# Turning -max one step later and putting four fill products behind the first key scores of a burst

## The chip, the cores and the metric

The kernel runs on one core of one Trainium2 chip. The metric is the device time of one execution, in microseconds (us); the times of before are three runs, and one more execution was recorded by the hardware profiler.

## The reference

Two independent results are joined along the last axis. Sequence length S is 2048, width D is 1024, there are 32 heads of width 32, and all heads share one set of keys and values. Everything is float32.

```python
# A: attention
q = (x @ wq).reshape(B, S, H, Dh).transpose(0, 2, 1, 3)
k = x @ wk
v = x @ wv
scores = einsum("bhqd,bkd->bhqk", q, k) * (Dh ** -0.5)
p = softmax(scores, axis=-1)
a = einsum("bhqk,bkd->bhqd", p, v).transpose(0, 2, 1, 3).reshape(B, S, H * Dh) @ wo
# B: Fourier mixing, real part
fa = einsum("bsd,ed->bse", xb, dft_hid_re);  fb = einsum("bsd,ed->bse", xb, dft_hid_im)
b = einsum("ts,bse->bte", dft_seq_re, fa) - einsum("ts,bse->bte", dft_seq_im, fb)
return concatenate([a, b], axis=-1)
```

## The kernel before

**Two streams on TensorE.** The attention proper is cut into 32 units (4 blocks of 512 queries times 8 groups of 4 heads) and each unit into 32 steps. All other matrix products (the projections of q, the Fourier part, the output projection) are the *fill*: float32 products made of three products of high and low halves each, `rh`/`rl` times `mh`/`ml`, 128x512 in size, written to the two one-bank PSUM pools that appear as `psb`. A group of 12 or 24 fill products adds up in one bank; when a group ends, VectorE copies or adds the bank out. `take(n)` issues the next n fill products, `pos["fill"]` counts them, and transfers and casts for later fill are issued when the count comes near their due position (`pump`).

**What one step does.** A step n of the main loop issues, in this order: `score_step(n + 44)`, `expo(n)`, and fill up to a level.

- `score_step` calls `ask`, which issues the *query scores* of a step 44 ahead (`scores`: two products `pss<-kst,qst` with the queries on the partitions, and VectorE's `TENSOR_REDUCE nm<-pss`, which gives -max per query), and ScalarE's exponential with row sums of the query scores before them (`pss<-pss,nm`). The pool `ps_s` of `pss` has two buffers.
- `expo(n)` issues the *key scores*: two products `pst<-qst,kst` with the keys on the partitions, and ScalarE's `p<-pst`, the exponential that the product with v needs. The pool `ps_t` of `pst` has one buffer, so the next key scores wait until this exponential has read it.
- At every eighth step (r % 8 == 0) three fill products, one more `ask`, and then `pv` follow: 16 products `psb<-p,v` with v (32 rows in the trace), into the `psb` bank that no open group holds, read out by VectorE (`ov`).

I call the eight steps from one `pv` to the next a *burst* and number the steps in it 0 to 7 (n % 8): `pv` ends step 0. T1, T2, T3 are the key scores of steps 1, 2 and 3. In step 1 no new query scores are issued, as step 0 has issued two sets.

**Turning -max.** The exponentials by keys need -max of each query as a row, which the query scores give as a column. Once a unit, `lse_1` to `lse_2` work it out on VectorE and ScalarE, `lse_3` turns it on TensorE (`psb<-ident,m`, one 48x128 product into a `psb` bank) and VectorE copies it out (`COPY mt<-psb`), and `lse_4` has SyncE send it into two rows of the unit's queries (`qst<-mt`) and the inverse sums to DRAM (`r<-mt`). `score_step` calls them by e, the number of steps since the last query scores of the unit. The loop is 12 steps ahead, so e = 5 falls on step 25 of a unit, which is step 1 of a burst, right behind `pv`.

**Ends of groups.** `aside()` stands ahead of `pv` and of the turning: when the open group is within six products of its beginning or its end, it issues the few products that bring it past that point, so that a bank is free.

**What sets the order.** The order on every engine is the order in which this Python code issues instructions (`keep_in_program_order`); each engine runs its own list in order, and waits by semaphores.

**Fill per step.** `level(n)` gives the fill position that must be reached by the end of a step: within a burst it is 3 at the `pv`, and from there a line up to w, the fill of one burst, over steps m = n % 8.

Of the kernel before, what the change touches and what calls it, by code (L numbers as in the profile page):

```python
# [87 lines left out]
def tile_kernel(ctx: ExitStack, tc, xT, wq, wkv, wo, xbT, wT, cT, out):  # L88
# [50 lines left out]
    class Line:  # L139
# [22 lines left out]
        def pump(self):  # L162
            for k in range(4):
                while self.may(k) and self.items[self.n[k]].due - self.lead[k] <= pos["fill"]:
                    self.step(k)
# [6 lines left out]
    pos = {"fill": 0, "s": 0}  # L172
# [90 lines left out]
    def add(gs):  # L263

        for g in gs:
            i0 = g.at = end[0]
            end[0] += g.n
            if groups and g.set[0] is not groups[-1].set[0]:
                prev["set"] = prev["this"]
                prev["this"] = i0  # L270
            for c, it in enumerate(g.right):
                if it.need is None:
                    it.need = i0 + 3 * c
                    p0 = prev["set"]
                    it.due = min(it.need, p0 + (i0 - p0) * (g.first + c + 1) // (len(g.set) * len(g.right)))
                    RL.items.append(it)
                it.last = i0 + 3 * c + 2
            for c, it in enumerate(g.left):
                if it.need is None:
                    it.need = it.due = i0 + 12 * c  # L280
                    ML.items.append(it)
                it.last = i0 + 12 * c + 11
            for it in g.ys:
                it.due = i0 + g.n
                ylist.append(it)
            groups.append(g)
# [14 lines left out]
    def at(p, f):  # L301
        k = len(later)
        while k and later[k - 1][0] > p:
            k -= 1
        later.insert(k, (p, f))

    def run_later():
        while later and later[0][0] <= pos["fill"]:
            later.pop(0)[1]()
# [18 lines left out]
    def bank(name, open_=False):  # L328

        b = 1 - cur["bank"] if cur["bank"] is not None else int(used[1] < used[0])  # L330
        cur["at"] += 1
        used[b] = cur["at"]
        if open_:
            cur["bank"] = b
        return ps_b[b].tile([P, W], F32, name=name)
# [10 lines left out]
    def product(g, ps, j):  # L346
        c, w = divmod(j, 3)
        l, r = g.left[c // 4], g.right[c]
        a = (l.lo if w == 2 else l.hi)[:, c % 4]
        te.matmul(ps[:g.rows], a, r.lo if w == 1 else r.hi, start=j == 0, stop=j == g.n - 1)  # L350

    def take(n):
        for _ in range(n):
            if cur["group"] >= len(groups):
                return
            g = groups[cur["group"]]
            j = pos["fill"] - g.at
            if j == 0:
                cur["ps"] = bank("psb", True)
            if j % 3 == 0:  # L360
                RL.force(g.right[j // 3])
            if j % 12 == 0:
                ML.force(g.left[j // 12])
            product(g, cur["ps"], j)
            pos["fill"] += 1
            if j == g.n - 1:
                cur["group"] += 1
                assert all(hasattr(it, "done") for it in g.ys)
                g.post(cur["ps"])
                cur["at"] += 1  # L370
                used[cur["bank"]] = cur["at"]
                cur["bank"] = None
                if g.ys:
                    at(pos["fill"] + 2 * BEHIND, lambda n=len(g.ys): yused.__setitem__(0, yused[0] + n))
            pump()
            run_later()

    def aside():

        if cur["group"] >= len(groups):  # L380
            return
        g = groups[cur["group"]]
        j = pos["fill"] - g.at
        if 0 < j < 6:
            take(6 - j)
        elif j > g.n - 6:
            take(g.n - j)
# [155 lines left out]
    def wo_set(e):  # L543
        return [Item([(lambda g=g: wo[g * P:(g + 1) * P, e * W:(e + 1) * W], 1)]) for g in range(NG)]
# [46 lines left out]
    def open_unit(u):  # L591
        b, g = units[u]
        assert ("q", b, g) in ready
        q = qsp.tile([P, 4, W], F32R, name="qst")
        gp.memset(q[96:P].bitcast(F32), 0.0)
        for r, src in enumerate((qh_d, ql_d, qh_d)):
            move(sp, q[r * DH:(r + 1) * DH], src[b][g].rearrange("(h d) c -> d h c", d=DH))
        qst[u] = q
        nm[u] = sm.tile([P, 2, NC], F32, name="nm")
        ls[u] = sm.tile([P, 2, NC], F32, name="ls")  # L600

    def scores(s):
        u, r = divmod(s, SU)
        i, j = divmod(r, 2)
        h, t = divmod(i, 4)
        ps = ps_s.tile([P, 2 * W], F32, name="pss")
        for a in range(2):
            k0 = (2 * j + a) * W
            te.matmul(ps[:, a * W:(a + 1) * W], qst[u][:, h, t * P:(t + 1) * P], kst[:, k0:k0 + W], start=True, stop=True)
        dve.tensor_reduce(nm[u][:, j, i:i + 1], ps, axis=AX.X, op=ALU.max, negate=True)  # L610
        pend[s] = ps

    def row_sums(s):
        if s not in pend:
            return
        ps = pend.pop(s)
        u, r = divmod(s, SU)
        i, j = divmod(r, 2)
        act.activation(ps, ps, AF.Exp, bias=nm[u][:, j, i:i + 1], accum_out=ls[u][:, j, i:i + 1])

    def lse_1(u):
        m = sm.tile([P, NC], F32, name="mm")
        d = sm.tile([P, 2, NC], F32, name="md")
        dve.tensor_tensor(m, nm[u][:, 0], nm[u][:, 1], op=ALU.min)
        for j in range(2):
            dve.tensor_sub(d[:, j], m, nm[u][:, j])
        lse[u] = m, d

    def lse_1b(u):
        act.activation(lse[u][1], lse[u][1], AF.Exp)  # L630

    def lse_2(u):
        m, d = lse[u]
        l = sm.tile([P, NC], F32, name="l")
        m2 = sm.tile([P, 3, NC], F32, name="m2")
        dve.tensor_mul(d, d, ls[u])
        dve.tensor_add(l, d[:, 0], d[:, 1])
        dve.tensor_copy(m2[:, 0].bitcast(F32R), m)
        dve.tensor_sub(m2[:, 1], m, m2[:, 0])
        dve.reciprocal(m2[:, 2], l)  # L640
        lse[u] = m2

    def lse_3(u):
        m2 = lse.pop(u)
        aside()
        pm = bank("psb")
        te.transpose(pm[:3 * NC, :P], m2.rearrange("p a b -> p (a b)"), ident)
        mt = sm.tile([3 * NC, P], F32, name="mt")
        dve.tensor_copy(mt, pm[:3 * NC, :P])
        cur["at"] += 1  # L650
        lse[u] = mt

    def lse_4(u):
        mt = lse.pop(u)
        for a in range(2):
            move(sp, qst[u][96 + a:97 + a].rearrange("o h (t c) -> o (h t) c", c=P), mt[a * NC:(a + 1) * NC])
        sp.dma_start(r_d[u], mt[2 * NC:])
# [47 lines left out]
    def ask(s):  # L705

        if s < total and s == asked[0]:
            asked[0] += 1
            u, r = divmod(s, SU)
            if r == SU - 6 and u + 1 < len(units):  # L710
                open_unit(u + 1)
            scores(s)
            row_sums(s - 1)
        else:
            row_sums(min(s, total - 1))

    def score_step(s):

        ask(s)
        u, e = divmod(s - SU, SU)  # L720
        if 0 <= u < len(units):
            if e == 1:
                lse_1(u)
            elif e == 2:
                lse_1b(u)
            elif e == 3:
                lse_2(u)
            elif e == 5:
                lse_3(u)
            elif e == 7:  # L730
                lse_4(u)


# [11 lines left out]
    for s in range(SU + LEAD):  # L745
        score_step(s)
        take(7)

    PRO = pos["fill"]
# [6 lines left out]
    def level(n):  # L756
        w = (FILL - PRO - LAST) / (total // 8)
        m = n % 8
        take(int(w * (n // 8) + (3 + (w - 3) * max(m - 1.5, 0) / 6.5 if m else 0)) + PRO - pos["fill"])

    for n in range(total):
        u, r = divmod(n, SU)
        if n == total - 12:
            w1 = wo_set(1)
            add([o_group(NQ - 1, t, e, ws) for e, ws in ((0, w0), (1, w1)) for t in range(4)])
        score_step(n + SU + LEAD)
        if ends:
            ends.pop(0)()
        expo(n)
        if r == 16:  # L770
            inverse(u)
        if r % 8 == 0 and n:
            take(3)
            ask(n + 1 + SU + LEAD)
            pv(*divmod(n // 8 - 1, 4))
        level(n + 1)
# [72 lines left out]
```

## Time and profile before

| | |
|---|---|
| three runs | 2915.01, 2915.35, 2917.73 us; median 2915.35 us |
| the profiled execution | 2913.28 us, span 2911.5 us from its first to its last instruction |
| mean granted TensorE clock | 0.999 |
| busy share of the span | PE (products) 97%, weight loads 66%, ScalarE 76%, VectorE 67%, GpSimd 42% |
| main loop, first to last key scores | from 163.0 us to about 2850 us of the span |

Times in the trace are microseconds from the span's start. A row of the timeline gives start, duration, engine, operation, output<-inputs, shapes and count, and in brackets the idle time of the engine just before it with what ended it. Rows of one kind that follow each other are merged ("x2" is the two halves of one 1024-wide score tile). TensorE's products are pipelined: one that lasts 0.39 us lets the next start 0.23 us later, so distances of starts are read, not durations. Line 66 is the helper that records every operation; groups are told apart by the names of their tiles.

### The profile page before, as it was taken

Reading aid. Unit: us, or ns where it says so; the run is one execution under the profiler, and the core shown is the slowest. Engines: PE = TensorE matmul, PEld = TensorE weight load, DVE = VectorE, ACT = ScalarE, POOL = GpSimd, SP = SyncE. Lnnn points to the kernel's source line nnn. Section 1 sums busy time; section 2 is a strip of 40 time slices with the busy share of each in tenths; the row PEclk is TensorE's granted clock in tenths of the full one; section 3 lists DMA queues with packets and bytes.
Section 4 is the critical chain, followed back from the end, with each engine's and each line's share of the span. In section 5 each row is a group of like instructions: output and inputs, shape, how many; then the busy total and the mean of one; then the engine's idle time right before and its main releaser. Section 6 shows DMA issues by size and latency. Waiting matters only on the chain.

```text
span 2911.5 us, 39943 instructions
## 1 busy us (share of the span) xinstructions
PE 2810.4 (97%) x13904; PEld 1920.2 (66%) x13904; DVE 1948.5 (67%) x2430; ACT 2206.6 (76%) x3151; POOL 1209.1 (42%) x928
## 2 busy tenths in 40 slices
PE   7999999999999999999999999999999999999999
PEld 5776666666666666666666666666666666666656
DVE  6876667677677766767776666777777766656511
ACT  4578888878787878888787878778778787888740
POOL 1211113544324336555563454776666653510000
PEclk9999999999999999999999999999999999999999
DMA  8855425665666455454452454564554542444345
GB/s 295 289 192 161 153 91 175 230 210 182 198 225 208 153 167 155 145 167 126 157 174 88 126 161 121 181 202 134 175 162 150 174 124 98 149 145 136 122 148 156
DMA packets 315722, 480.83 MB, mean 165 GB/s; under 512 B 33408, under 2 KB 98432, under 8 KB 315520
## 3 DMA queue, kind: packets, MB, share of 16 engines
q1 hardware_dynamic: 315520, 478.28, 51.6%
q8 instruction: 109, 1.79, 0.3%
q14 instruction: 93, 0.76, 0.1%
HBM read 364.12 MB, written 112.98 MB: 164 GB/s over the span
## 4 chain that ended last, share of the span: by engine, by line
PE 83%; DVE 5%; ACT 5%; DMA 3%; issue 2%; POOL 2%; SPq 1%; POOLq 0%; ACTq 0%; DVEq 0%
PE psb L66 52%; PE pst L66 17%; PE pss L66 14%; ACT p L66 4%; DVE nm L66 2%; ACT pss L66 1%; DVE rh L66 1%; DVE mh L66 1%; SPq L66 1%; DVE ov L66 1%; POOL ml L66 1%; POOL m L66 1%; DMA r<-s 1%; DMA p<-in_xT_dram 0%; DMA ql<-ql 0%
## 5 line engine op out<-in xcount | busy, mean ns | idle before, releaser
L66 DVE TENSOR_REDUCE nm<-pss 128x1 f32<-128x1024 f32 x1024 | 1247.4, 1221 | 481.7 <-PE pss L66 478.0
L66 ACT ACTIVATE p<-pst 128x1024 f32<-128x1024 f32 x1024 | 1051.4, 1027 | 445.4 <-PE pst L66 440.7
L66 ACT ACTIVATE pss<-pss,nm 128x1024 f32<-128x1024 f32 x1024 | 1113.1, 1087 | 175.4 <-DVE nm L66 166.8
L66 PE MATMUL psb<-rh,mh 128*128 128x512 f32 (+1 forms) x1852 | 730.2, 394 | 11.0 <-ACT rh L66 8.3
L66 PE MATMUL psb<-rh,ml 128*128 128x512 f32 (+1 forms) x1852 | 729.7, 394 | 0.7 <-POOL ml L66 0.7
L66 PE MATMUL psb<-rl,mh 128*128 128x512 f32 (+1 forms) x1852 | 729.3, 394 | 0.3 <-DVE rl L66 0.3
L66 PE MATMUL pst<-qst,kst 128*128 128x512 f32 x2048 | 677.9, 412 | 47.3 <-ACT p L66 46.7
L66 PE MATMUL pss<-kst,qst 128*128 128x512 f32 x2048 | 644.9, 396 | 12.9 <-ACT pss L66 12.4
L66 POOL TENSOR_TENSOR rl<-r,rh 128x512 fp32r<-128x512 f32 x214 | 279.6, 1307 | 763.3 <-DVE rh L66 560.2
L66 POOL TENSOR_TENSOR ml<-m,mh 128x512 fp32r<-128x512 f32 x292 | 382.4, 1310 | 514.7 <-DVE mh L66 242.8
L66 PEld LDWEIGHTS pst<-qst,kst 128*128 128x128 f32 x2048 | 357.7, 188 | 272.2 <-ACT p L66 131.2
L66 PE MATMUL psb<-p,v 128*32 128x512 f32 x4096 | 466.0, 595 | 2.1 <-DVE y L66 2.1
L66 PEld LDWEIGHTS pss<-kst,qst 128*128 128x128 f32 x2048 | 382.1, 188 | 112.2 <-ACT pss L66 24.7
L66 PEld LDWEIGHTS psb<-rh,mh 128*128 128x128 f32 (+1 forms) x1852 | 346.8, 187 | 97.9 <-ACT rh L66 9.0
L66 PEld LDWEIGHTS psb<-rl,mh 128*128 128x128 f32 (+1 forms) x1852 | 346.7, 187 | 84.8 <-DVE rl L66 1.4
L66 PEld LDWEIGHTS psb<-rh,ml 128*128 128x128 f32 (+1 forms) x1852 | 346.6, 187 | 84.3 <-POOL ml L66 1.1
L66 PEld LDWEIGHTS psb<-p,v 128*32 128x32 f32 x4096 | 120.0, 109 | 278.7 <-issue 251.9
L66 POOL TENSOR_TENSOR m<-m,m 128x512 f32<-128x512 f32 x192 | 253.2, 1319 | 7.2 <-DMA m<-in_cT_dram 6.5
L66 POOL TENSOR_TENSOR r<-r,r 128x512 f32<-128x512 f32 x112 | 149.1, 1331 | 214.2 <-DMA r<-in_wT_dram 119.9
L66 DVE TENSOR_TENSOR ov<-ov,psb 128x512 f32<-128x512 f32 x96 | 65.9, 687 | 228.8 <-PE psb L66 228.7
L66 ACT ACTIVATION_READ_ACCUMULATOR pss<-pss,nm 128x1 f32 x1024 | 206.5, 202 | 0.0
L66 DVE CAST mh<-m 128x512 fp32r<-128x512 f32 x291 | 164.2, 564 | 15.1 <-POOL m L66 7.1
(68 smaller groups left out, 841.1 us busy)
## 6 DMA issues: line engine op xcount, KB each, us to landing
m<-in_cT_dram SPq DMA_DIRECT2D x384, 256.0 KB, 3.7
r<-s SPq DMA_DIRECT2D x192, 256.0 KB, 4.3
y<-y SPq DMA_DIRECT2D x96, 256.0 KB, 4.4
r<-in_wT_dram SPq DMA_DIRECT2D x80, 256.0 KB, 3.7
m<-in_xbT_dram SPq DMA_DIRECT2D x80, 256.0 KB, 4.1
y<-u SPq DMA_DIRECT2D x80, 256.0 KB, 2.8
qst<-qh SPq DMA_DIRECT2D x64, 256.0 KB, 5.7
s<-y SPq DMA_DIRECT2D x64, 256.0 KB, 2.8
```

What stands on the lines that cost most here:

```text
L66: return lambda *a, **k: self.tc.keep_in_program_order(f(*a, **k))
```

## The change

Three things are moved; nothing is added to the work or taken from it.

1. `lse_3` (the turning) is called at e = 6 instead of 5, and `lse_4` (its transfers) at e = 8 instead of 7. The turning falls on step 2 of a burst, between its query scores and its key scores.
2. `level`: the line of fill within a burst starts at m = 1.3 instead of 1.5, and behind T1 at least four fill products are issued.
3. At the eighth steps `aside()` is also called before the additional `ask`, so the few products that it issues stand ahead of the second query scores and no longer between them and `pv`.

```diff
-            elif e == 5:
+            elif e == 6:
                 lse_3(u)
-            elif e == 7:
+            elif e == 8:
                 lse_4(u)
...
     def level(n):
         w = (FILL - PRO - LAST) / (total // 8)
         m = n % 8
-        take(int(w * (n // 8) + (3 + (w - 3) * max(m - 1.5, 0) / 6.5 if m else 0)) + PRO - pos["fill"])
+        f = int(w * (n // 8) + (3 + (w - 3) * max(m - 1.3, 0) / 6.7 if m else 0)) + PRO - pos["fill"]
+        take(max(f, 4) if m == 2 else f)
...
         if r % 8 == 0 and n:
             take(3)
+            aside()
             ask(n + 1 + SU + LEAD)
             pv(*divmod(n // 8 - 1, 4))
```

The order on TensorE in the 40th burst, from the last product with v on; `psb` with `rh`/`rl` is fill, `pst` key scores (T1, T2, T3), `pss` query scores. Before:

```order
L66 MATMUL psb_9430<-p_9391,v_316 32x512 x2
L66 MATMUL pst_9453<-qst_8201,kst_313 128x512 x2
L66 MATMUL psb_9407<-rh_8640,mh_9291 128x512
L66 MATMUL pss_9458<-kst_313,qst_8974 128x512 x2
L66 MATMUL pst_9464<-qst_8201,kst_313 128x512 x2
L66 MATMUL psb_9407<-rl_8641,mh_9291 128x512
```

And after, at the same place:

```order
L66 MATMUL psb_9448<-p_9398,v_316 32x512 x2
L66 MATMUL pst_9471<-qst_8208,kst_313 128x512 x2
L66 MATMUL psb_9475<-rh_8910,mh_9278 128x512
L66 MATMUL psb_9475<-rl_8911,mh_9278 128x512
L66 MATMUL psb_9475<-rh_8910,ml_9279 128x512
L66 MATMUL psb_9475<-rh_9021,mh_9278 128x512
L66 MATMUL pss_9481<-kst_313,qst_8981 128x512 x2
L66 MATMUL pst_9487<-qst_8208,kst_313 128x512 x2
L66 MATMUL pss_9491<-kst_313,qst_8981 128x512 x2
L66 MATMUL pst_9498<-qst_8208,kst_313 128x512 x2
L66 MATMUL psb_9475<-rl_9022,mh_9278 128x512
```

Between T1 and T2 stood one fill product, now four; between T2 and T3 stood six, now none, since the level of step 3 had already been passed.

The order on TensorE in the 19th burst, where a unit's -max is turned (`psb<-ident,m2`). Before, it follows the products with v at once:

```order
L66 MATMUL psb_5359<-p_5305,v_316 32x512 x2
L66 MATMUL psb_5378<-ident_308,m2_5299 48x128
L66 MATMUL pst_5383<-qst_3574,kst_313 128x512 x2
L66 MATMUL pss_5387<-kst_313,qst_5064 128x512 x2
L66 MATMUL pst_5392<-qst_3574,kst_313 128x512 x2
L66 MATMUL psb_5396<-rh_4089,mh_5184 128x512
```

After:

```order
L66 MATMUL psb_5359<-p_5318,v_316 32x512 x2
L66 MATMUL pst_5379<-qst_3585,kst_313 128x512 x2
L66 MATMUL psb_5383<-rh_4079,mh_5146 128x512
L66 MATMUL psb_5383<-rl_4080,mh_5146 128x512
L66 MATMUL psb_5383<-rh_4079,ml_5147 128x512
L66 MATMUL psb_5383<-rh_4177,mh_5146 128x512
L66 MATMUL pss_5388<-kst_313,qst_5068 128x512 x2
L66 MATMUL psb_5383<-rl_4178,mh_5146 128x512
L66 MATMUL psb_5383<-rh_4177,ml_5147 128x512
L66 MATMUL psb_5394<-ident_308,m2_5312 48x128
L66 MATMUL pst_5399<-qst_3585,kst_313 128x512 x2
```

The turning moved from its place behind the products with v to one behind T1, four products, the query scores and the two products of its own `aside()`.

The order on VectorE at the same place; `ov` reads the bank of the products with v, `mt` is the copy of the turned -max, `nm` the maximum of query scores, `y0` the read-out of a group's bank. Before:

```order
L66 TENSOR_REDUCE nm_5069<-pss_5344 128x1
L66 TENSOR_TENSOR y0_5234<-y0_5234,psb_5314 128x512
L66 TENSOR_TENSOR ov_4967<-ov_4967,psb_5359 128x512
L66 COPY mt_5380<-psb_5378 48x128
L66 TENSOR_REDUCE nm_5069<-pss_5387 128x1
```

After:

```order
L66 TENSOR_TENSOR y0_5234<-y0_5234,psb_5297 128x512
L66 TENSOR_REDUCE nm_5073<-pss_5354 128x1
L66 TENSOR_TENSOR ov_4967<-ov_4967,psb_5359 128x512
L66 TENSOR_REDUCE nm_5073<-pss_5388 128x1
L66 COPY mt_5396<-psb_5394 48x128
```

The copy of the turned -max now stands behind the maximum of step 2's query scores, and a group that `aside()` ends is read out ahead of the maximum of the additional query scores.

## The prediction

> **What bounds the kernel now.** I read the page first, then who waits for whom on TensorE, then the timeline of one burst.
>
> ```profile
> span 2911.5 us, 39943 instructions
> ...
> PE 2810.4 (97%) x13904; PEld 1920.2 (66%) x13904; DVE 1948.5 (67%) x2430; ACT 2206.6 (76%) x3151; POOL 1209.1 (42%) x928
> ...
> PE 83%; DVE 5%; ACT 5%; DMA 3%; issue 2%; POOL 2%; SPq 1%; POOLq 0%; ACTq 0%; DVEq 0%
> ```
>
> TensorE's products cover 97% of the span and carry 83% of the chain that ended last. The change removes no product, so it can only win what TensorE loses between products. These are its longest waits that the place of the change could touch:
>
> ```profile
> PE pst L66 <- ACT p L66: 46.7, 108, 1.3
> PE psb L66 <- DVE ov L66: 17.9, 21, 1.3
> PE pss L66 <- ACT pss L66: 12.4, 14, 4.3
> ```
>
> The first is key scores that wait for ScalarE to read the one `pst` buffer, the second the turning that waits for VectorE to read the bank of the products with v. They are idle time only; the modelled ends of products hide more, so I measure from start to start. One burst, on TensorE and ScalarE:
>
> ```profile
> 1005.71 3.64 PE L66 MATMUL psb<-p,v 128*32 128x512 f32 x32
> ...
> 1009.28 0.73 PE L66 MATMUL pst<-qst,kst 128*128 128x512 f32 x2
> ...
> 1009.85 0.40 PE L66 MATMUL psb<-rh,mh 128*128 128x512 f32 x1
> ...
> 1010.04 1.02 ACT L66 ACTIVATE p<-pst 128x1024 f32<-128x1024 f32 x1 [1.94 <-PE pst L66]
> 1010.08 0.63 PE L66 MATMUL pss<-kst,qst 128*128 128x512 f32 x2
> ...
> 1011.12 0.73 PE L66 MATMUL pst<-qst,kst 128*128 128x512 f32 x2 [0.41 <-ACT p L66]
> ...
> 1011.69 0.40 PE L66 MATMUL psb<-rl,mh 128*128 128x512 f32 x1
> ...
> 1011.92 0.39 PE L66 MATMUL psb<-rh,ml 128*128 128x512 f32 x1
> ...
> 1013.07 0.63 PE L66 MATMUL pss<-kst,qst 128*128 128x512 f32 x2
> ...
> 1013.53 0.63 PE L66 MATMUL pst<-qst,kst 128*128 128x512 f32 x2
> ...
> 1014.20 1.03 ACT L66 ACTIVATE p<-pst 128x1024 f32<-128x1024 f32 x1 [0.20 <-PE pst L66]
> ...
> 1015.12 1.08 ACT L66 ACTIVATE pss<-pss,nm 128x1024 f32<-128x1024 f32 x1
> ...
> 1016.29 1.03 ACT L66 ACTIVATE p<-pst 128x1024 f32<-128x1024 f32 x1
> ```
>
> From it come the unit prices. A fill product takes 0.23 us (1011.69 to 1011.92). Query scores take 0.46 (1013.07 to 1013.53), key scores that did not wait about the same. Key scores that waited take 0.57 (1009.28 to 1009.85, 1011.12 to 1011.69), 0.10 more. ScalarE starts its exponential 0.67 after key scores that did not wait (1013.53 to 1014.20) and 0.76 after ones that did; it needs 1.03, and the next key scores start 0.06 later (10.04 + 1.02 to 11.12). So two key scores cannot stand closer than 1.84 us behind a wait, or 1.76 without one. ScalarE alone needs 2.09 us a step (1014.20 to 1016.29).
>
> T1 always follows the products with v, so it always has the long start. Here T1 to T2 took 1.84 with one product between. With none and with three it is the same:
>
> ```profile
> 1030.87 0.73 PE L66 MATMUL pst<-qst,kst 128*128 128x512 f32 x2
> ...
> 1032.72 0.73 PE L66 MATMUL pst<-qst,kst 128*128 128x512 f32 x2 [0.65 <-ACT p L66]
> ...
> 1033.28 0.40 PE L66 MATMUL psb<-rh,mh 128*128 128x512 f32 x1
> ```
>
> ```profile
> 1114.97 0.74 PE L66 MATMUL pst<-qst,kst 128*128 128x512 f32 x2
> ...
> 1116.83 0.74 PE L66 MATMUL pst<-qst,kst 128*128 128x512 f32 x2
> ...
> 1117.40 0.39 PE L66 MATMUL psb<-rh,mh 128*128 128x512 f32 x1
> ```
>
> 1.85 and 1.86, and 2.41 and 2.43 to the next fill product. Up to three products there are free: they stand where TensorE waits anyway.
>
> **Term 1, four products behind T1: -69 us.** Four products make 0.57 + 4 x 0.23 + 0.46 = 1.95 us from T1 to T2, 0.11 more than the 1.84 that the exponential asks for; T2 then doesn't wait and takes 0.47. That is 2.42 to the next product, as before, with more work in it. In the order of instructions, 123 bursts of before have 0, 1, 2 or 3 products there in 42, 13, 29 and 39 cases; all of after have four or more. Missing to four: 42 x 4 + 13 x 3 + 29 x 2 + 39 = 304 products, times 0.23 is 70 us, less 123 x 0.01. This is not less work but work moved into a wait, and it is earned only if the later steps become shorter by what has left them.
>
> **Term 2, the turning: -18 us.** A turning of before that waits:
>
> ```profile
> 1069.38 3.64 PE L66 MATMUL psb<-p,v 128*32 128x512 f32 x32
> ...
> 1073.08 0.69 DVE L66 TENSOR_TENSOR ov<-ov,psb 128x512 f32<-128x512 f32 x1 [3.44 <-PE psb L66]
> ...
> 1073.83 0.29 PE L66 MATMUL psb<-ident,m 128*48 128x128 f32 x1 [0.81 <-DVE ov L66]
> ...
> 1073.87 0.70 PE L66 MATMUL pst<-qst,kst 128*128 128x512 f32 x2
> 1074.15 0.28 DVE L66 COPY mt<-psb 48x128 f32<-48x128 f32 x1 [0.39 <-PE psb L66]
> ...
> 1074.46 1.15 SPq L66 DMA_DIRECT2D qst<-mt  x2
> ...
> 1088.54 0.63 PE L66 MATMUL pst<-qst,kst 128*128 128x512 f32 x2
> ```
>
> T1 starts 4.49 us behind the first product with v; in the burst above, without a turning, 3.57. The turning itself is 0.05 (1073.83 to 1073.87), so its wait costs 0.87, in the 21 cases of the second wait row: 18 us. At the new place the bank was read before: `ov` ends 0.8 us behind the place that T1 has without a turning (1073.77 against 1069.38 + 3.57), and the turning comes at least 0.57 + 0.92 + 0.46 = 1.95 us behind T1.
>
> **Term 3, what is late next: +36 us.** The fill level is a fixed line, so what is issued early is missing at step 3. Between T2 and T3 after has 0, 1, 2, 3 products in 19, 13, 15, 11 bursts (before never under 3). TensorE needs 0.93 + 0.23 for each, the exponential 1.76: it waits 0.83, 0.60, 0.37, 0.14. That is 15.8 + 7.8 + 5.6 + 1.5 = 30.7, and 0.10 each for T3 that waited, 58 x 0.10 = 5.8. ScalarE does nothing between the exponentials of T1 and T2 (no query scores were issued in step 1), so the price is not larger.
>
> [...]
>
> **Term 4, the shorter later steps: +5 us.** Steps 3 to 7 hold 5.5 products each before and 5.3 after; 0.17 x 0.23 x 5 x 123 = 24 us leave them. On TensorE a step is then 0.93 + 5.3 x 0.23 = 2.15 us, still over ScalarE's 2.09. But ScalarE is sometimes late itself, because VectorE is:
>
> ```profile
> ACT pss L66 <- DVE nm L66: 166.8, 208, 20.0
> ...
> L66 DVE TENSOR_REDUCE nm<-pss 128x1 f32<-128x1024 f32 x1024 | 1247.4, 1221 | 481.7 <-PE pss L66 478.0
> L66 DVE CAST mh<-m 128x512 fp32r<-128x512 f32 x291 | 164.2, 564 | 15.1 <-POOL m L66 7.1 <-DMA m<-in_wq_dram 7.1 <-DMA ql<-ql 0.4
> ```
>
> 208 of 1024 steps: a fifth of the 24 us is not earned. Bounds: 0 (or some less than nothing, as VectorE's casts are issued with the fill and move away too) and all 24.
>
> **Term 5, banks behind the turning: +4 us.** In five bursts the new `aside()` ends a group at the turning, and the next group at once needs the bank that VectorE reads out behind the maximum of step 2. From the end of those query scores that is 1.22 + 0.69 (a read-out like `ov`) = 1.9 us, of which two or three products and the key scores fill 1.0: about 0.9 us each. Bounds 0 and 8.
>
> **Term 6, the additional query scores: -2 us.** The products of `aside()` now stand ahead of them and give ScalarE time to free the `pss` buffer; the third wait row bounds the gain at 12 us and includes other places. The group that it ends is read ahead of their maximum, one or two read-outs of 0.69 us; the 3.57 us of products with v cover both the maximum and its exponential, else T1's exponential would be late by as much.
>
> **At nothing.** `lse_4`'s transfers start a step later. They started at 1074.46 and the unit's first key scores at 1088.54, 14 us later:
>
> ```profile
> L66 SPq DMA_DIRECT2D qst<-mt x64: 518/555/1562, 149.9 to 2765.8; - x64
> ...
> DMA to landing us min/median/max: 1.6/1.8/3.9
> ```
>
> They land in at most 3.9 us; a step of 2.1 and the turning's later place leave some 10. If that cover were gone, each missing microsecond would cost 31 times. SyncE stands at this transfer until the turning is copied, with later loads of fill behind it; its distance of two steps from the turning is kept, so it waits no longer than before. GpSimd's list moves only with the fill.
>
> **Sum:** -69 - 18 + 36 + 5 + 4 - 2 = -44 on the profiled execution's 2913.3 us, 2869 us. The median of the runs is 2 us above that execution: **2871 us**.
>
> **The rivals.**
>
> *The later steps don't shorten.* If ScalarE and VectorE set steps 3 to 7, moved fill earns nothing, and term 3 has nothing to take either: only the turning is won, 2915 - 18 = 2897 us. For it: the 208 late steps. Against it: ScalarE waited 0.20 for TensorE at 1014.20, and a step of after is above its 2.09. [...] A half of this rival is 2884 us.
>
> *The turning's wait goes with it.* Between query and key scores it might wait for another bank as it did for `ov`: term 2 is nothing, 2889 us. Against it: the bank that it takes was last read by `ov`, 1.1 us earlier by the distances of term 2.
>
> *Slower: VectorE's list.* If each turning of after met a bank read out behind step 2's maximum, it would wait 1.22 + 0.69 = 1.9 us, 31 x 1.9 = 59 us: 2871 + 59 = 2930. It decides from 23 turnings on (44 / 1.9). The order shows a group ended at the turning in a handful only, and there it is the fill behind it that meets this bank.
>
> **How the numbers follow.** The forecast, with its own range of 2854 to 2886 from the bounds of terms 4 to 6, has 0.72. The later steps in whole or half have 0.14, the turning's wait 0.08, the slower case 0.02, better than the forecast's range 0.04 (T3's waits met by casts that have moved away). The range 2854 to 2890 takes in the forecast, the turning's case and half the first rival. A measurement of this kernel tells 0.2% (6 us) from no change; all cases but the last lie further below, so faster has 0.95, same 0.03 for mixtures of the rivals, slower 0.02.
>
> **What the profile of after would show.** Key scores of step 2 without a wait (T1 to T2 1.95 us), the wait row of `psb` for `ov` gone, waits for `p` in some 58 bursts, now at T3 and at most 0.8 us each, steps 3 to 7 of about 2.15 us. Wrong would be: longer waits of `pss` for its buffer, of fill for a bank, or of T4 and later for `p`.

## The result: 2894 us, faster than before by half of what was forecast

| | before | changed kernel |
|---|---|---|
| runs taken beside each other | 2914.91 us (2911.97 to 2917.73, 6 runs) | 2894.31 us (2892.52 to 2897.29, 6 runs) |
| ratio | | 0.9931, 95% interval 0.9918 to 0.9944 |
| the profiled execution | 2913.28 us, span 2911.5 | 2892.52 us, span 2890.7 |
| mean granted TensorE clock | 0.999 | 0.996 |

Forecast were 2871 us and a range of 2854 to 2890. The gain is 20.6 us instead of 44. Two runs of the experiments below stand apart: one of the four of `after_pro494` took 6540.11 us and is left out of its time and ratio, and one of the six of `turn_pro494` took 2916.40 us at a mean granted clock of 0.948 (the others 2895.74 to 2900.33) and is kept.

From the page of the changed kernel (the span, the busy times, the chain that ended last by engine):

```profile
span 2890.7 us, 39942 instructions
...
PE 2804.9 (97%) x13904; PEld 1920.9 (66%) x13904; DVE 1956.4 (68%) x2430; ACT 2195.2 (76%) x3151; POOL 1208.8 (42%) x928
...
PE 79%; DVE 5%; issue 4%; ACT 4%; DMA 3%; POOL 3%; SPq 1%; POOLq 0%; ACTq 0%; DVEq 0%
```

TensorE is still the bound, but the chain leaves it more often. From the list of waits of the changed kernel (engine and line that waited, what ended it: idle us in total, times, longest):

```profile
ACT pss L66 <- DVE nm L66: 234.0, 226, 20.5
...
PE pst L66 <- ACT p L66: 30.6, 73, 1.8
PE pss L66 <- ACT pss L66: 27.5, 19, 4.7
DVE mh L66 <- POOL m L66: 20.0, 17, 2.4
```

The key scores' wait fell from 46.7 to 30.6 us and the turning's row (17.9, 21 times) is gone from the top of the list, as forecast. Three other rows grew: the exponentials of query scores wait 234.0 us for their maxima instead of 166.8, the query scores wait 27.5 us for their buffer instead of 12.4, and VectorE's casts `mh<-m` wait 20.0 us for GpSimd's sums `m<-m,m`, before 7.1 (in the `CAST` row that the prediction quoted).

When the loop begins and ends is read from the first and last start of the products `pst` (duration min/median/max ns, first and last start). Before, then the changed kernel:

```profile
L66 PE MATMUL pst<-qst,kst x2048: 387/397/507, 163.0 to 2850.2; 128*128 128x512 f32 x187
```

```profile
L66 PE MATMUL pst<-qst,kst x2048: 387/397/658, 167.1 to 2829.4; 128*128 128x512 f32 x187
```

The loop lasts 2687.2 and 2662.3 us, so it became 24.9 us shorter, and it begins 4.1 us later.

**The two intended gains are there.** A burst of the changed kernel, on TensorE and ScalarE (timeline: start, duration, engine, operation, idle before it and what ended it):

```profile
437.15 0.74 PE L66 MATMUL pst<-qst,kst 128*128 128x512 f32 x2
437.73 0.39 PE L66 MATMUL psb<-rh,mh 128*128 128x512 f32 x1
...
438.42 0.40 PE L66 MATMUL psb<-rh,mh 128*128 128x512 f32 x1
438.65 0.63 PE L66 MATMUL pss<-kst,qst 128*128 128x512 f32 x2
439.12 0.62 PE L66 MATMUL pst<-qst,kst 128*128 128x512 f32 x2
439.58 0.63 PE L66 MATMUL pss<-kst,qst 128*128 128x512 f32 x2
...
439.78 1.02 ACT L66 ACTIVATE p<-pst 128x1024 f32<-128x1024 f32 x1 [0.82 <-PE pst L66]
...
440.86 0.73 PE L66 MATMUL pst<-qst,kst 128*128 128x512 f32 x2 [0.65 <-ACT p L66]
...
441.43 0.40 PE L66 MATMUL psb<-rl,mh 128*128 128x512 f32 x1
```

Four products fill the time from T1 (437.15) to T2 (439.12): 1.97 us, no wait, forecast 1.95. T3, with no fill between, starts 1.74 behind T2 and waits 0.65 idle: that is the forecast's "late next". And a turning:

```profile
397.72 0.39 PE L66 MATMUL psb<-rh,ml 128*128 128x512 f32 x1
397.95 0.27 PE L66 MATMUL psb<-ident,m 128*48 128x128 f32 x1
397.98 0.71 PE L66 MATMUL pst<-qst,kst 128*128 128x512 f32 x2
```

It starts 0.23 behind the product ahead of it, so it waits for no bank.

**Where the rest was lost.** The largest single idle time of TensorE in the changed kernel's loop, and the engines behind it, VectorE, GpSimd, ScalarE and TensorE in order of time (`h` is the read-out of a finished group, `y<-y,h` and `m<-m,m` are GpSimd's sums of halves of the Fourier part, `mh` the high half of the result as the next fill needs it):

```profile
1819.84 0.68 DVE L66 TENSOR_TENSOR h<-h,psb 128x512 f32<-128x512 f32 x1
...
1820.59 2.54 POOL L66 TENSOR_TENSOR y<-y,h 128x512 f32<-128x512 f32 x2 [6.23 <-DVE h L66]
...
1821.01 1.23 DVE L66 TENSOR_REDUCE nm<-pss 128x1 f32<-128x1024 f32 x1 [0.50 <-PE pss L66]
...
1823.09 1.29 POOL L66 TENSOR_TENSOR m<-m,m 128x512 f32<-128x512 f32 x1
...
1824.41 1.49 DVE L66 CAST mh<-m 128x512 fp32r<-128x512 f32 x1 [2.18 <-POOL m L66]
...
1825.83 1.49 DVE L66 CAST rh<-r 128x512 fp32r<-128x512 f32 x1
...
1825.92 0.39 PE L66 MATMUL psb<-rh,ml 128*128 128x512 f32 x1
...
1827.24 2.34 DVE L66 TENSOR_REDUCE nm<-pss 128x1 f32<-128x1024 f32 x2
...
1828.55 1.09 ACT L66 ACTIVATE pss<-pss,nm 128x1024 f32<-128x1024 f32 x1 [3.96 <-DVE nm L66]
...
1829.81 0.73 PE L66 MATMUL pss<-kst,qst 128*128 128x512 f32 x2 [3.50 <-ACT pss L66]
...
1830.47 5.34 PE L66 MATMUL psb<-p,v 128*32 128x512 f32 x32
```

The same work in the kernel before:

```profile
1841.80 0.69 DVE L66 TENSOR_TENSOR h<-h,psb 128x512 f32<-128x512 f32 x1
...
1842.56 2.54 POOL L66 TENSOR_TENSOR y<-y,h 128x512 f32<-128x512 f32 x2 [4.79 <-DMA y<-y]
...
1842.95 1.22 DVE L66 TENSOR_REDUCE nm<-pss 128x1 f32<-128x1024 f32 x1 [0.46 <-PE pss L66]
...
1845.04 1.22 DVE L66 TENSOR_REDUCE nm<-pss 128x1 f32<-128x1024 f32 x1 [0.86 <-PE pss L66]
...
1846.39 1.50 DVE L66 CAST mh<-m 128x512 fp32r<-128x512 f32 x1
...
1847.82 1.51 DVE L66 CAST rh<-r 128x512 fp32r<-128x512 f32 x1
...
1849.25 1.21 DVE L66 TENSOR_REDUCE nm<-pss 128x1 f32<-128x1024 f32 x1
```

In both the cast starts some 4.6 us behind the read-out, since GpSimd has three sums to do in between. Before, VectorE's list has two maxima in that time and the cast then finds its input just ready (the sum ends at 1846.36). In the changed kernel it has one maximum and then the cast; VectorE stands 2.18 us, and the maximum that comes behind the two casts starts at 1827.24. ScalarE stands 3.96 us for it, the `pss` buffer comes free late, and TensorE starts nothing from 1825.92 to 1829.81.

The tail of it is in the windows of TensorE (busy us, number of instructions, granted clock, DMA share, GB/s), ahead of, behind and beyond that idle time:

```profile
1826.40:1830.50 4.10, 0.69 (x6) 1.00 0.73 255
1830.70:1833.90 3.20, 3.20 (x20) 0.50 0.72 207
1834.10:1837.70 3.60, 3.60 (x24) 1.00 0.61 235
```

Behind the idle time the clock is at half for a while, and the products with v take 5.34 instead of 3.64 us. The changed kernel has three such stretches in the loop (from 1830.6, 1878.4 and 1922.8), the profile before has none.

Why the cast stands elsewhere: in the prologue of the loop, which runs the same steps ahead of the first key scores, the moved turning now falls where its `aside()` issues four products of fill more. The fill's position at the first key scores is 498, before 494, and the whole line of fill, which `level` reckons from that position (`PRO`), is moved by four products at the loop's start, less later and nothing at the end. Groups end elsewhere against the steps. In the order on VectorE, among the casts `mh<-m` that follow a read-out `h<-h,psb` with only maxima and casts of `r` between, 6 had one maximum and 23 two; in the changed kernel 14 have one and 14 two.

### The profile page after: what moved, and what is told of

Read it like the earlier page. It is cut to its first block, busy times and chain, and to the rows that moved or that the text cites. A ratio compares the mean times of both kernels' runs of the same rounds, so it can differ in the third digit from the quotient of the medians.

```text
span 2890.7 us, 39942 instructions
## 1 busy us (share of the span) xinstructions
PE 2804.9 (97%) x13904; PEld 1920.9 (66%) x13904; DVE 1956.4 (68%) x2430; ACT 2195.2 (76%) x3151; POOL 1208.8 (42%) x928
## 4 chain that ended last, share of the span: by engine, by line
PE 79%; DVE 5%; issue 4%; ACT 4%; DMA 3%; POOL 3%; SPq 1%; POOLq 0%; ACTq 0%; DVEq 0%
PE psb L66 50%; PE pst L66 15%; PE pss L66 14%; ACT p L66 2%; DVE nm L66 2%; DMA r<-s 1%; ACT pss L66 1%; POOL ml L66 1%; SPq L66 1%; DVE rh L66 1%; DVE mh L66 1%; POOL m L66 1%; DMA ql<-ql 1%; DMA m<-in_cT_dram 1%; DMA r<-in_xT_dram 0%
## 5 line engine op out<-in xcount | busy, mean ns | idle before, releaser
L66 DVE TENSOR_REDUCE nm<-pss 128x1 f32<-128x1024 f32 x1024 | 1247.1, 1221 | 468.8 <-PE pss L66 466.1
L66 ACT ACTIVATE p<-pst 128x1024 f32<-128x1024 f32 x1024 | 1052.7, 1028 | 372.2 <-PE pst L66 367.6
L66 ACT ACTIVATE pss<-pss,nm 128x1024 f32<-128x1024 f32 x1024 | 1114.2, 1088 | 241.0 <-DVE nm L66 234.0
L66 PE MATMUL psb<-rh,mh 128*128 128x512 f32 (+1 forms) x1852 | 731.5, 395 | 17.0 <-ACT rh L66 8.9
L66 PE MATMUL psb<-rh,ml 128*128 128x512 f32 (+1 forms) x1852 | 730.1, 394 | 0.7 <-POOL ml L66 0.7
L66 PE MATMUL psb<-rl,mh 128*128 128x512 f32 (+1 forms) x1852 | 729.8, 394 | 0.3 <-DVE rl L66 0.3
L66 PE MATMUL pst<-qst,kst 128*128 128x512 f32 x2048 | 675.5, 411 | 31.8 <-ACT p L66 30.6
L66 PE MATMUL pss<-kst,qst 128*128 128x512 f32 x2048 | 646.3, 396 | 28.0 <-ACT pss L66 27.5
L66 POOL TENSOR_TENSOR rl<-r,rh 128x512 fp32r<-128x512 f32 x214 | 279.5, 1306 | 751.6 <-DVE rh L66 508.9
L66 POOL TENSOR_TENSOR ml<-m,mh 128x512 fp32r<-128x512 f32 x292 | 383.1, 1312 | 500.7 <-DVE mh L66 242.8
L66 PEld LDWEIGHTS pst<-qst,kst 128*128 128x128 f32 x2048 | 353.0, 188 | 271.6 <-ACT p L66 106.3
L66 PE MATMUL psb<-p,v 128*32 128x512 f32 x4096 | 468.5, 598 | 0.1
L66 PEld LDWEIGHTS pss<-kst,qst 128*128 128x128 f32 x2048 | 382.6, 188 | 128.3 <-ACT pss L66 40.9
L66 PEld LDWEIGHTS psb<-rh,mh 128*128 128x128 f32 (+1 forms) x1852 | 347.3, 188 | 104.8 <-ACT rh L66 9.4
L66 PEld LDWEIGHTS psb<-rl,mh 128*128 128x128 f32 (+1 forms) x1852 | 347.1, 187 | 84.7 <-DVE rl L66 1.8
L66 PEld LDWEIGHTS psb<-rh,ml 128*128 128x128 f32 (+1 forms) x1852 | 347.1, 187 | 84.4 <-POOL ml L66 1.1
L66 PEld LDWEIGHTS psb<-p,v 128*32 128x32 f32 x4096 | 120.4, 110 | 278.9 <-issue 257.7
L66 POOL TENSOR_TENSOR m<-m,m 128x512 f32<-128x512 f32 x192 | 253.6, 1321 | 10.4 <-DMA m<-in_cT_dram 6.7
L66 POOL TENSOR_TENSOR r<-r,r 128x512 f32<-128x512 f32 x112 | 147.3, 1315 | 189.5 <-DMA r<-in_wT_dram 96.5
L66 DVE TENSOR_TENSOR ov<-ov,psb 128x512 f32<-128x512 f32 x96 | 66.0, 687 | 219.2 <-PE psb L66 219.2
L66 ACT ACTIVATION_READ_ACCUMULATOR pss<-pss,nm 128x1 f32 x1024 | 208.8, 204 | 0.0
L66 DVE CAST mh<-m 128x512 fp32r<-128x512 f32 x291 | 170.1, 584 | 27.7 <-POOL m L66 20.0
```

The costliest lines, as they stand in the source:

```text
L66: return lambda *a, **k: self.tc.keep_in_program_order(f(*a, **k))
```

## The experiments

My theory: the moved line of fill costs the missing time, through VectorE's casts. Rivals: the turning costs at its new place (banks, T3), or the steps 3 to 7 can't become shorter and there is nothing more to win. Each kernel was timed beside the kernel before, on the same chip; "loop" is last less first start of `pst`, as above.

| kernel | fill ahead | time, us | before | ratio (95%) | `pst` first, last | loop |
|---|---|---|---|---|---|---|
| changed kernel | 498 | 2894.31 | 2914.91 | 0.9931 (0.9918 to 0.9944) | 167.1, 2829.4 | 2662.3 |
| turn_only | 498 | 2917.29 | 2915.47 | 1.0008 (0.9999 to 1.0017) | 166.4, 2854.2 | 2687.8 |
| level_only | 494 | 2884.62 | 2915.47 | 0.9891 (0.9878 to 0.9905) | 160.5, 2819.0 | 2658.5 |
| aside_only | 494 | 2914.15 | 2915.47 | 0.9995 (0.9986 to 1.0004) | 164.4, 2851.1 | 2686.7 |
| after_comb40 | 498 | 3037.49 | 2915.47 | 1.0415 (1.0401 to 1.0430) | 168.1, 2973.9 | 2805.8 |
| turn_pro494 | 494 | 2899.72 | 2916.06 | 0.9951 (0.9933 to 0.9968) | 160.5, 2837.1 | 2676.6 |
| before_pro498 | 498 | 2930.78 | 2916.06 | 1.0050 (1.0038 to 1.0062) | 162.5, 2867.1 | 2704.6 |
| after_pro494 | 494 | 2875.98 | 2916.06 | 0.9866 (0.9849 to 0.9884) | 161.2, 2811.1 | 2649.9 |
| after_cast24 | 498 | 2881.53 | 2916.06 | 0.9880 (0.9868 to 0.9893) | 166.4, 2816.3 | 2649.9 |
| after_pro490 | 490 | 2873.98 | 2916.98 | 0.9852 (0.9838 to 0.9867) | 161.1, 2809.8 | 2648.7 |
| after_494_cast24 | 494 | 2875.38 | 2916.98 | 0.9861 (0.9845 to 0.9878) | 162.0, 2809.9 | 2647.9 |

**The change in its parts.** The turning alone:

```diff
-            elif e == 5:
+            elif e == 6:
                 lse_3(u)
-            elif e == 7:
+            elif e == 8:
                 lse_4(u)
```

> Of the three parts only the turning of -max is moved (e = 6 and 8); the fill line and aside() are those of before. Theory (VectorE held by GpSimd): the turning's wait for `ov` is gone, 21 waits of 0.87 us, so 2915 - 19 = about 2896 us, with the wait row of `psb` for `ov` near nothing and the waits of T2 for `p` as before. Rival (the turning waits as long at its new place): 2915 us, no change.

The level alone:

```diff
-        take(int(w * (n // 8) + (3 + (w - 3) * max(m - 1.5, 0) / 6.5 if m else 0)) + PRO - pos["fill"])
+        f = int(w * (n // 8) + (3 + (w - 3) * max(m - 1.3, 0) / 6.7 if m else 0)) + PRO - pos["fill"]
+        take(max(f, 4) if m == 2 else f)
```

> Of the three parts only the fill line with at least four products behind T1; 0, 1, 2, 3 products are left between T2 and T3 in 12, 12, 14, 15 bursts. Theory (the moved fill is earned, and what is lost is lost in a few places where VectorE stands behind GpSimd's combination of `m`): -69 for T2, +30 for T3, +5 to +10 for these places, as the order has them 8 times with one maximum between `h` and the cast, 6 before: 2878 to 2886 us. Rival (steps 3 to 7 in general don't shorten, ScalarE and VectorE set them): 2900 to 2915 us, with the lost time spread over all bursts.

And `aside()` ahead of the additional query scores alone:

```diff
         if r % 8 == 0 and n:
             take(3)
+            aside()
```

> Of the three parts only the aside() ahead of the additional query scores. Theory: 0 to -5 us (2910 to 2915), the products of aside() give ScalarE time to free the `pss` buffer. Rival (a group's bank is read ahead of the maximum of the additional scores, their exponential comes late and T1's with it): +3 to +10 us, with longer waits of `p` in step 1.

Alone, the third part does nothing that can be told. The level alone is better than the whole change: its ratio is 0.0040 lower, which is 12 us of 2915. The turning alone brings nothing, although its wait, 17.9 us, is gone: the time is the rival's, but not for the rival's reason. Its list of waits shows what came instead:

```profile
PE pss L66 <- ACT pss L66: 24.3, 15, 4.4
...
DVE mh L66 <- POOL m L66: 15.0, 12, 2.4
```

Both rows are near those of the changed kernel (27.5 and 20.0); `level_only`, which stays at 494, has 12.2 and 8.1 there. The turning itself needs neither `pss` nor `mh`.

**GpSimd's sum earlier.** In the changed kernel, the second lead of the line of `m` (products ahead of use at which the sum is issued) from 36 to 40, the first (its loads) with it:

```diff
-    ML = Line(NM0, NM, (52, 36, 27, 21), load_m, comb, hi_m, lo)
+    ML = Line(NM0, NM, (56, 40, 27, 21), load_m, comb, hi_m, lo)
```

> The changed kernel, but GpSimd's combination of `m` is issued 40 products ahead of its use and its loads 56 (36 and 52 in after), that is 4 products before a group ends and so ahead of the additions to `y` that wait for the end of that group. The cast stays at 27. Theory: VectorE's wait for `m` (20.0 us in after) falls under 5 us, the waits of query scores for their buffer from 27.5 to about 10 us, the three stretches of half clock around 1830 to 1925 us go, and the time falls from 2894 to 2872 to 2880 us. Rival (shorter steps in general are not earned): 2890 to 2896 us.

It failed as a probe. The waits that it should have taken away became seven times as long:

```profile
POOL r L66 <- DMA r<-s: 402.4, 64, 10.3
...
DVE mh L66 <- POOL m L66: 141.4, 38, 9.1
```

GpSimd stands on the other factor's input `r` (402.4 us, in the changed kernel and its parts 76 to 90), which comes over the same queue (SyncE issues `r<-s` right behind `m<-in_cT_dram`, at 1942.53 and 1941.68 us), and its sums for `m` stand behind it. So two things were changed at once, loads and sums, and the run says only that both together, four products earlier, make the kernel slower.

**The line of fill by itself.** The turning alone, with four products fewer ahead of the first key scores and given back behind the prologue's steps, so that the position is 494 again:

```diff
-    take(66)
+    take(62)
...
+    take(4)
```

> turn_only again, but with the fill line where before has it: the turning's aside() in the steps ahead of the main loop had put four more products ahead of it (498 instead of 494), which moved the whole line by four products at the start of the loop. Here take(66) is take(62) and four products are taken behind those steps, 494 again. Theory (the turning wins its 19 us, and the moved line loses them where VectorE's cast meets GpSimd's combination of `m`): 2897 to 2905 us, VectorE's wait for `m` back from 15 to about 7 us. Rival (the turning itself gives its gain back, by banks and by key scores of step 3): 2914 to 2918 us, wait for `m` as in turn_only.

The kernel before with four products more ahead (498) and nothing of the change:

```diff
-    take(66)
+    take(70)
```

> The kernel before, with nothing of the change, but with take(70) for take(66): four more products ahead of the loop, the line of fill where the changed kernel has it. Theory: slower by 8 to 18 us, 2923 to 2933, VectorE's wait for `m` rises from 7 to about 15 us, stretches of half clock appear around 1460 to 2100 us. Rival (the position of the line means nothing): 2915 us.

And the whole change with 494, by the same edit as `turn_pro494`:

> The changed kernel with all three parts and with the line of fill at 494, as in before. Theory: what level_only won (31 us) and most of the turning's 19 us: 2870 to 2878 us, VectorE's wait for `m` from 20 to about 8 us. Rival: 2890 to 2896 us, as after.

`before_pro498` is slower than before by 14.7 us, with the signature of the changed kernel, and without any part of the change:

```profile
PE pss L66 <- ACT pss L66: 21.1, 13, 3.5
...
DVE mh L66 <- POOL m L66: 16.8, 13, 2.4
```

The count of casts with one maximum goes along: 10 in `before_pro498` and `turn_only`, 8 in `level_only` and `after_pro494`, 6 in `turn_pro494`, `aside_only` and before. The turning alone at 494 gains 16.3 us, and the whole change at 494 gains 40.1. In `after_pro494` the query scores and the casts are back near the 12.4 and 7.1 us of before, and the key scores keep their gain:

```profile
PE pst L66 <- ACT p L66: 31.3, 76, 1.4
...
PE pss L66 <- ACT pss L66: 14.5, 18, 2.1
...
DVE mh L66 <- POOL m L66: 8.5, 10, 2.5
```

The row of exponentials that wait for maxima is still at 213.0 us there (before 166.8), and at 211.4 in `aside_only`, whose time did not change; so its growth by itself is not the loss.

So the line of fill costs 15 us without the change (ratio 1.0050), 17 with the turning (1.0008 against 0.9951) and 19 with the whole change (0.9931 against 0.9866), each difference times 2915 us.

**The casts by themselves.** The line stays at 498, but the cast of `m` is issued twelve instead of nine products behind the sum (third and fourth lead):

```diff
-    ML = Line(NM0, NM, (52, 36, 27, 21), load_m, comb, hi_m, lo)
+    ML = Line(NM0, NM, (52, 36, 24, 18), load_m, comb, hi_m, lo)
```

> The changed kernel with its line at 498, but VectorE's cast of `m` is issued 24 products ahead of its use and GpSimd's low half 18 (27 and 21 in after): twelve products behind the combination instead of nine. Theory: VectorE finds `m` ready, its wait falls from 20 to under 8 us, the half clock stretches go, 2868 to 2880 us. Rival (the loss is not in this wait): 2890 to 2896 us. If the low half now comes late for TensorE, fill waits for `ml` and it is slower than 2896.

The loop lasts 2649.9 us, as in `after_pro494`, with the line still at 498, from an edit that moves only the casts of `m` and GpSimd's low halves behind them. Its waits:

```profile
PE pss L66 <- ACT pss L66: 8.2, 13, 3.4
DVE mh L66 <- POOL m L66: 8.1, 3, 4.7
```

The casts still wait as long as in `after_pro494`, but in 3 places instead of 10. The 5.6 us by which the kernel is slower than `after_pro494` lie ahead of the loop, which begins 5.2 us later (166.4 against 161.2); so its time came out just above the expected range. Against my expectation the half clock did not go: the loop has three stretches again (from 1874.2, 2048.2 and 2072.1), and still is 12.4 us shorter than that of the changed kernel. So these 12.4 us were not lost by half clock.

**Both, and four products fewer still.** `after_494_cast24` has both edits; `after_pro490` has `take(62)` without the `take(4)`:

> The changed kernel with the line of fill put back (494 ahead of the first key scores) and with the casts of the second factor twelve instead of nine products behind GpSimd's combination. Theory: both edits remove the same waits of VectorE for GpSimd, so they do not add up: 2870 to 2879, the clock at 0.998 or more. Rival (they act on different losses, -17 and -13 against the changed kernel's 2894): 2864.

> The changed kernel with four fill products fewer ahead of the main loop and none given back (490 ahead of the first key scores, against 494 before and 498 in the changed kernel; those four are earned back over the loop). Theory (it is the place of the casts against the maxima on VectorE's list, not a count of products): the order has one maximum between read-out and cast 6 times, as before the change, so VectorE's waits for GpSimd stay at 7 to 10 us and the time at 2877, within 6 us. Rival (each four products that are moved ahead of the loop cost some 16 us by themselves): 2861.

The two edits don't add up: 2875.38 us, loop 2647.9 against 2649.9 for either; its mean granted clock, 0.997 to 0.998, was just under what I expected. And four products fewer still are worth 4 us by the two ratios (0.9852 against 0.9866, intervals overlapping), not 16. Its order has 7 casts with one maximum, not 6, and they waited 12.1 us, more than I expected; the query scores 17.1. So the row of waits alone doesn't rank the kernels. All four kernels with the whole change and without the shift's effect on the casts meet at loops of 2648 to 2650. `after_pro490` is the fastest kernel here, 0.9852 of before and by the ratios 23 us faster than the change as it was made; its lead over `after_pro494` and `after_494_cast24` is within their intervals.

## Why the prediction was wrong

To set the terms beside the traces I took, for each pair of neighbouring products in the loop, the distance of their starts beyond 0.232 us (0.048 behind a turning; 0.523 behind the last product with v, 0.327 ahead of the first; pairs within these left out), and summed it by the step in which it lies:

| lost in the loop, us | before | changed kernel | after_pro494 | forecast for the difference |
|---|---|---|---|---|
| step 0 (`pv`, turning before) | 30.1 | 13.1 | 7.1 | -18 - 2 (terms 2, 6) |
| steps 1 to 3 | 90.6 | 66.4 | 64.4 | -69 + 36 + 4 (terms 1, 3, 5) |
| steps 4 to 7 | 22.1 | 36.8 | 34.0 | +5 (term 4) |
| sum | 142.8 | 116.4 | 105.6 | -44 |

- **Terms 1 and 3 (four products, T3 late next): right in mechanism, near in size.** Steps 1 to 3 lost 24.2 us less, forecast 29 with term 5. T1 to T2 has no wait, T3 has it: 0.65 idle in the burst above. 73 waits of key scores instead of some 58, the longest 1.8 instead of 0.8.
- **Term 2 (the turning): right.** The wait is gone; in three bursts the key scores behind the turning waited 0.5 to 1.6 us instead; at 494 the turning alone gains 16.3 us of the 18. "The turning's wait goes with it" is out.
- **Term 5 (banks): right.** Five bursts of the changed kernel have fill that waits for a bank behind the turning, 0.8 to 1.5 us each, 5.2 us in all; forecast five times 0.9.
- **"At nothing": "GpSimd's list moves only with the fill" is the step that failed.** It moved with the fill, and the prediction didn't ask how far the fill moved, or what stands behind it on VectorE. I had compared the orders inside the loop only. The moved turning's `aside()` in the prologue shifts the loop's whole line. Steps 0 to 7 lose 10.8 us more with it (116.4 against 105.6), the loop is 12.4 us longer (2662.3 against 2649.9; the pairs left out of the table, products with v, took 5.34 instead of 3.64 us once at half clock), and the loop begins 5.9 us later (167.1 against 161.2). By the spans that is 18.3 us (2890.7 against 2872.4). Of the later beginning four products are 0.9. Another 1.8 us is term 5 once more, in the prologue: behind the moved turning (started at 152.59) fill waits for the bank that VectorE is reading out.

  ```profile
  154.47 0.50 PE L66 MATMUL psb<-rh,mh 128*128 128x512 f32 x1 [1.61 <-DVE ql L66]
  ```

  All four kernels that move the turning and keep `take(66)` have this wait and begin at 166.4 to 168.1; the other eight begin at 160.5 to 164.4. The rest of the 5.9 us, some 3, is not settled.
- **Term 4 (shorter later steps): mis-sized, +5 forecast, +12 measured without the shifted line.** The loss of steps 4 to 7 rises from 22.1 to 34.0 in `after_pro494` (36.8 in the changed kernel), 10.3 of these 11.9 us in steps 6 and 7. The prediction named the sign, "longer waits of `pss` for its buffer", and scaled it by the share of steps with a late maximum. Its mean step of 2.15 us hides a mixture: in `after_pro494` 56% of the steps 4 to 7 last 2.09 or less from start to start (before 47%), which is ScalarE's own 2.09. But this mixture alone does not make the term 12: in `after_494_cast24`, with the casts moved, the share is the same and steps 4 to 7 lose 25.2, 3 more than before, while steps 1 to 3 lose 72.1 instead of 64.4. So where the casts stand decides which steps lose the time; the sum stays (103.7 against 105.6). Why it stays was not tested.
- **Half clock: not in the sum at all.** Three stretches of 3.4 us at half clock lose 1.7 each (half of 3.41, an estimate), about 5 us, contained in the numbers above; `after_pro494` has one.
- **"The later steps don't shorten" (2897) came out at nearly the measured time and is still wrong**: the level alone gains 30.9 us, and the whole change 40.1 with the line put back. That time, 2876, lies within the forecast's own range of 2854 to 2886. "Slower: VectorE's list" put its price on the turning's copy. The wait on VectorE's list was real, though it was casts and not copies.

## What to carry to other kernels

A step that is moved also moves in the prologue, and there it can shift everything that is counted from the prologue's end: compare the orders at the loop's first instruction, and the counters that it starts from, before pricing anything inside the loop. Where an engine that runs its list in order has an operation on another engine's result, count how much of its other work stands between the request and that operation; one item fewer turned a hidden latency of 4.6 us into a wait of 2.2 and an idle time of 3.5 two engines further. When a gain comes out at a fraction, run each part alone, and then the suspected side effect alone in the kernel before: `before_pro498` settled here what no reading of the changed trace could.

## What the runs showed of the hardware

**Half clock behind an idle time.** Each of the three stretches in the changed kernel lasts 3.41 us in the trace's clock record and follows an idle time of TensorE, of 3.50, 2.84 and 2.96 us. They begin 47.8 and 44.4 us behind each other, which is 14 and 13 times 3.41; why is not shown here. The length of one idle time doesn't decide alone. In the changed kernel this one was followed by none:

```profile
1452.73 0.50 PE L66 MATMUL pss<-kst,qst 128*128 128x512 f32 x1 [2.86 <-ACT pss L66]
```

and in `after_pro494` a shorter one was:

```profile
1839.19 0.90 PE L66 MATMUL pss<-kst,qst 128*128 128x512 f32 x2 [1.78 <-ACT pss L66]
```

```profile
1839.70:1842.90 3.20, 3.19 (x8) 0.50 0.85 257
```

So idle times of 3.50, 2.96, 2.84 and 1.78 us were followed by half clock in these two traces, and one of 2.86 us was not. What decides it was not tested.

**Casts beside GpSimd.** The casts at 1824.41 and 1825.83, and those of before at 1846.39 and 1847.82, took 1.49 to 1.51 us while GpSimd worked; the one at 1817.75 in the changed kernel, with GpSimd idle, took 0.42:

```profile
1817.75 0.42 DVE L66 CAST mh<-m 128x512 fp32r<-128x512 f32 x1
```

So this pair of casts cost VectorE 2.1 us more beside GpSimd, as much as a whole step. In the kernel before, from the first key scores to the end of the span, none of the 285 casts of `m` and `r` (128x512) that no GpSimd instruction overlapped by more than 0.01 us took over 0.43 us, and of the 194 others 60 took over 1 us, up to 2.11. The changed kernel has 73 over 1 us, `before_pro498` 56. So `before_pro498` did not lose its 14.7 us by more slow casts; they matter where a maximum stands behind them, as with ScalarE's 3.96 us above.
